# Retention and a mixture of experts on one core: other SBUF places for x and the first weights, and the two parts of an expert's first layer in two runs

## The chip, the cores and the metric

The kernel runs on one NeuronCore of a Trainium2 chip. Its time is the time of one execution on the device, in microseconds (us). The median of three executions before the change is 603.05 us (602.06 to 604.78).

The engines have short names here, as in the profile: PE is TensorE's matmul, PEld its load of the stationary operand, DVE is VectorE, ACT is ScalarE, POOL is GpSimd, SP is the queue that starts most DMA transfers.

## What is computed

The reference takes q, k and v of 8 batches, 8 heads, 576 positions and 64 channels. It computes retention, and sends each of the 4,608 resulting rows of 512 values through one of eight experts, the one whose gate logit is largest.

```
scores = scale * q @ k.T                     # per batch and head
ret = scores * Dmat                          # gamma ** (i - j) for i >= j, else 0
x = (ret @ v), heads side by side            # (4608, 512)

logits = x @ w_gate                          # (4608, 8)
e_idx = argmax(logits)
gate_w = softmax(logits)[e_idx]
eom = sigmoid(x @ w_output_gate)
for e in range(8):
    mask = e_idx == e
    h = maximum(x[mask] @ w1[e], 0.0)        # w1[e] is 512 x 1024
    ye = h @ w2[e]                           # w2[e] is 1024 x 512
    out[mask] = gate_w[mask] * eom[mask, e] * ye
```

## The kernel before

**Two stages.** The first, up to about 160 us, computes retention in 36 tiles of 128 rows and scatters the finished rows of x into a table in DRAM, sorted by expert. The second runs the eight experts. Each expert has room for 616 rows (`CAP`), in two parts: part 0 of 360 rows (`CA`) and part 1 of 256. Rows over 616 would go through a loop at the end.

**Numbers in two halves.** Every operand of an expert's matmuls is split into a high and a low half in a 32-bit format that one pass of PE takes (`F32R`): `xh` and `xl`, `w1h` and `w1l`, and so on. A product is the sum of three matmuls: high by high, and the two mixed ones.

**The first layer.** `mm1(e, part, fb)` makes block `fb` of 128 of the 1,024 hidden columns, for one part of expert `e`: four slices `k` of the 512 inputs by three products, 12 matmuls into one PSUM tile `h_ps`. The stationary operand is 128 columns of a first-weight tile; the moving operand is x transposed, 360 columns in part 0 and 256 in part 1. ACT then makes `hh`, the high half of the rectified result (L275), and DVE `hl`, its low half (L276). There are four buffers of `h_ps`.

**The second layer.** `mm2(e, t)` makes one of five row tiles (three of part 0, with 128, 128 and 104 rows, two of part 1): 24 matmuls, the hidden rows stationary, 512 columns of the second weights moving (L289). ACT scales the result (L294) and POOL scatters it into the output.

**Order.** The second stage is written out by hand, and each engine keeps the order of the code. For each expert after the first, sixteen `mm1` blocks alternate between the parts, then five `mm2` follow. Expert 0's part 0 runs ahead of the loop (L664 to L671, L753), so that its loop has only the eight blocks of part 1. Into the loop over `fb` are set: the loads, casts and subtractions of this expert's second weights (`load_w(2, ...)`), the loads of the next expert's x (`load_x`) and row numbers (`load_idx`), and half of the next expert's first weights; the other half and the transposes of x (`transp_hi`, DVE's L245) are set between the `mm2`. Weights are staged in three buffers `st`, x in five buffers `x_q`. SP takes all these loads in one queue, and a load waits there for its buffer.

**Places in SBUF.** A matmul reads two operands from SBUF: the moving one, and the next matmul's stationary one, which PEld loads meanwhile. Each is a run of 4-byte numbers in each partition. All tiles of a kind begin at the same place within 256 bytes, since their sizes and the slices are multiples of 256 B. In the built program the bytes are, modulo 256: first weights 128, second weights 64, x of part 0 64, x of part 1 64, hidden tiles of both parts 64. So x begins 64 B below the first weights (192 modulo 256) in both parts, and the second weights at the same place as the hidden tiles (0). Three unused tiles called `shift` set these places; before the change there are two of them, `shift1` of 192 B between first and second weights (L139) and `shift2` of 128 B ahead of x's first part (L161).

Of the kernel before, what the change touches and what calls it, by code (L numbers as in the profile page):

```python
# [10 lines left out]
F32 = mybir.dt.float32  # L11
# [15 lines left out]
P = 128  # L27
# [12 lines left out]
FB = F // P  # L40
# [8 lines left out]
def tile_retention_moe(  # L49
# [20 lines left out]
    wpool = ctx.enter_context(tc.tile_pool(name="wpool", bufs=1))  # L70
# [58 lines left out]

    W1, W2 = {}, {}

    def start_w(which, e, fp):
        src, shape = (w1, [P, KB, 256]) if which == 1 else (w2, [P, 2, DM])
        st = wst.tile(shape, F32, name="st")
        SP.dma_start(out=st, in_=src[e, fp].rearrange("p (a b) -> p a b", a=shape[1]))
        if which == 2 and not W2:
            wpool.tile([P, 48], F32, name="shift1")  # L139
        hi = wpool.tile(shape, F32R, name=f"w{which}h{fp}")  # L140
        lo = wpool.tile(shape, F32R, name=f"w{which}l{fp}")
        (W1 if which == 1 else W2)[e, fp] = (hi, lo)
        return st, hi, lo

    def hi_w(st, hi, lo):
        for h in range(2):
            k = slice(h * st.shape[1] // 2, (h + 1) * st.shape[1] // 2)
            A.copy(out=hi[:, k], in_=st[:, k])  # L148

    def lo_w(st, hi, lo, part=range(2)):  # L150
        for h in part:
            k = slice(h * st.shape[1] // 2, (h + 1) * st.shape[1] // 2)
            V.tensor_tensor(out=lo[:, k], in0=st[:, k], in1=hi[:, k].bitcast(F32), op=ALU.subtract)  # L153

    def load_w(which, e, fp):
        w = start_w(which, e, fp)
        hi_w(*w)
        lo_w(*w)
# [6 lines left out]
    pools = {"xt0": xta, "ht0": hpa}  # L165
# [14 lines left out]
    def load_x(e, t):  # L180

        XG[e, t] = pools["xq"].tile([P, 4, P], F32, name="x_q")
        o = e * NT + ROW0[t]
        for a in range(4):
            read(paced=e == 1 and a == 0, out=XG[e, t][32 * a:32 * a + 32],
                 in_=xs[o:o + P, P * a:P * a + P].rearrange("(u j) c -> j u c", u=4))

    def load_idx(e, part, first=None):
        ts = range(TA) if part == 0 else range(TA, CT)
        if e == 0 and part == 0:  # L190
            for t in ts:
                o, m = ROW0[t], ROWS[t]
                read(first=first, out=idx[0:m, e, t], in_=xs[o:o + m, DM:DM + 2].bitcast(I32))
        else:
            o = e * NT + ROW0[ts[0]]
            read(out=idx[:, e, ts[0]:ts[-1] + 1],
                 in_=xs[o:o + P * len(ts), DM:DM + 2].rearrange("(t p) w -> p t w", p=P).bitcast(I32))
# [29 lines left out]
    def transp(e, t):  # L227
        transp_lo(*transp_hi(e, t))

    def transp_hi(e, t):  # L230
        part, n = (0, TA * P) if t < TA else (1, CAP - CA)
        t0 = t if part == 0 else t - TA
        if (e, part) not in XT:
            pl = pools[f"xt{part}"]
            XT[e, part] = (pl.tile([P, KB, n], F32R, name=f"xh{part}"), pl.tile([P, KB, n], F32R, name=f"xl{part}"))
        m = ROWS[t] if e == 0 else P
        hi, lo = (a[:, :, P * t0:P * t0 + m] for a in XT[e, part])
        if e == 0:
            src = pools["x_ps"]()[:, :, :, 0:m]
            for k in range(KB):  # L240
                T.transpose(src[:, k // 2, k % 2, :], XG[e, t][0:m, k:DM:KB], ident[0:m, 0:m])
            hi, lo = (a.rearrange("p (b k) i -> p b k i", b=2) for a in (hi, lo))
        else:
            src = pools["xq"].tile([P, KB, P], F32, name="x_t", bufs=2)
            V.transpose(out=src.rearrange("p k (u j) -> p u k j", u=4),  # L245
                        in_=XG[e, t].rearrange("p u (i k) -> p u k i", k=KB))
        A.copy(out=hi, in_=src)
        return src, hi, lo

    def transp_lo(src, hi, lo):  # L250
        V.tensor_tensor(out=lo, in0=src, in1=hi.bitcast(F32), op=ALU.subtract)

    def mm1(e, part, fb):
        hidden(*mm1_products(e, part, fb))

    def mm1_products(e, part, fb):
        n = CA if part == 0 else CAP - CA
        xh, xl = XT[e, part]
        wh, wl = (a[:, :, P * (fb % 2):P * (fb % 2) + P] for a in W1[e, fb // 2])
        w = -(-n // P) * P  # L260
        hh = pools[f"ht{part}"].tile([P, w], F32R, name=f"hh{part}{fb}")[:, 0:n]
        hl = pools[f"ht{part}"].tile([P, w], F32R, name=f"hl{part}{fb}")[:, 0:n]
        HT[e, part, fb] = (hh, hl)
        ps = pools["ps_h"].tile([P, 512], F32, name="h_ps")[:, 0:n]
        j = 0
        for k in range(KB):
            for a, b in ((wh, xh), (wh, xl), (wl, xh)):
                i = T.matmul(ps, lhsT=a[:, k, :], rhs=b[:, k, 0:n], start=(j == 0), stop=(j == 3 * KB - 1))  # L268
                if j == 0:
                    pe[0] = i.ins  # L270
                j += 1
        return ps, hh, hl

    def hidden(ps, hh, hl):
        A.activation(out=hh, in_=ps, func=AF.Relu)  # L275
        V.scalar_tensor_tensor(out=hl, in0=ps, scalar=0.0, in1=hh.bitcast(F32), op0=ALU.max, op1=ALU.subtract)  # L276

    def mm2(e, t):
        part = 0 if t < TA else 1
        t0 = t if part == 0 else t - TA  # L280
        m = ROWS[t]
        n = slice(P * t0, P * t0 + m)
        ps = pools["ps_y"].tile([P, DM], F32, name="y_ps")[0:m]
        j = 0
        for fb in range(FB):
            wh, wl = (a[:, fb % 2, :] for a in W2[e, fb // 2])
            hh, hl = HT[e, part, fb]
            for a, b in ((hh, wh), (hh, wl), (hl, wh)):
                i = T.matmul(ps, lhsT=a[:, n], rhs=b, start=(j == 0), stop=(j == 3 * FB - 1))  # L289
                if j == 0:  # L290
                    pe[0] = i.ins
                j += 1
        y = pools["y"].tile([P, DM], F32, name="y")[0:m]
        A.activation(out=y, in_=ps, func=AF.Copy, scale=idx.bitcast(F32)[0:m, e, t, 1:2])  # L294
        G.indirect_dma_start(out=out, out_offset=bass.IndirectOffsetOnAxis(ap=idx[0:m, e, t, 0:1], axis=0),  # L295
                             in_=y, in_offset=None, bounds_check=NT - 1, oob_is_err=False)
# [268 lines left out]
    def weights(g):  # L565
        for w, at in wsched.items():
            if g == at[0]:
                wparts[w] = start_w(w[0], 0, w[1])
            if g == at[1]:
                hi_w(*wparts[w])  # L570
# [170 lines left out]
    def fill_slots(e):  # L741
        for f in fills[e]:
            G.memset(iw, 0.0)
            f()
# [18 lines left out]
    load_x(1, 1)  # L763
    for e in range(E):
        nx = e + 1 < E
        for fb in range(FB):
            if e > 0:
                mm1(e, 0, fb)
            mm1(e, 1, fb)
            if e > 0 and fb < 4:  # L770
                load_w(2, e, fb)
            if e == 0:

                if fb in (0, 2):
                    w.append(start_w(1, 1, 2 + fb // 2))
                if fb in (1, 3, 5):
                    load_x(1, 2 + fb // 2)
                if fb % 2 == 1:
                    hi_w(*w[fb // 2])
                    lo_w(*w[fb // 2])  # L780
            elif nx:
                if fb < CT:
                    load_x(e + 1, fb)
                if fb in (5, 6):
                    load_idx(e + 1, fb - 5)
                if fb in (5, 7):
                    load_w(1, e + 1, (fb - 5) // 2)
            if fb == (7 if e else 4) and e + 2 < E:
                fill_slots(e + 2)
        if e == E - 1:  # L790
            overflow_table()
        xw = {}
        for t in range(CT):
            if e > 0 or t >= TA:

                for u in range(CT) if e == 0 and t == TA else (t,) if e else ():
                    if nx:
                        xw[u] = transp_hi(e + 1, u)
                        if u > 0:
                            transp_lo(*xw[u - 1])  # L800
                        if u == CT - 1:
                            transp_lo(*xw[u])
                if e and nx and t in (1, 3):
                    load_w(1, e + 1, 2 + t // 2)
                mm2(e, t)
# [3 lines left out]
    with ExitStack() as octx:  # L809
# [3 lines left out]
        with tc.For_i(0, n, 1) as i:  # L813
            e = nc.values_load(ovt[0:1, 0, bass.ds(i, 1)], engines=[mybir.EngineType.SP], min_val=0, max_val=E - 1)
# [106 lines left out]
```

## Time and profile before

| | |
|---|---|
| median of three executions | 603.05 us |
| the profiled execution's own time | 606.21 us |
| its span, first to last instruction | 604.4 us |
| granted TensorE clock, mean | 0.997 |
| retention stage | up to about 159.5 us |
| experts | 159.5 to about 597.2 us |
| matmuls of the first layer (L268) | 1,536 |
| matmuls of the second layer (L289) | 960 |

The page gives busy time by engine. For matmuls that is not enough: they overlap, and each has a duration longer than its distance to the next. What a matmul costs is that distance, from its start to the start of the next one, called its pitch below. It is read from the timeline, in which each row is an instruction with its start, its duration and its operands.

### The profile page before, as it was taken

The numbers are of one execution on the slowest core, as the hardware profiler recorded it, in microseconds if no ns is written. First come the engines' busy times: TensorE is split into PE (matmuls) and PEld (weight loads), VectorE is DVE, ScalarE is ACT, GpSimd is POOL, SyncE is SP. The second block draws the span as 40 slices with busy tenths as digits, with TensorE's granted clock in tenths as the row PEclk, the third lists the DMA queues.
The fourth block names the chain that finished last, engine by engine and source line by source line (L and its number), as shares of the span: only waits on it lengthen the run. The fifth ranks groups of instructions, "written<-read, shape, count | busy, mean of one in ns | idle before, by whom it ended". The sixth has DMA issues, their size and how long they took to land. (4 is left out here: it accounts for less than half of the span.)

```text
span 604.4 us, 14010 instructions
## 1 busy us (share of the span) xinstructions
PE 593.0 (98%) x5692; PEld 530.2 (88%) x5692; DVE 330.5 (55%) x731; ACT 226.0 (37%) x502; POOL 189.1 (31%) x235
## 2 busy tenths in 40 slices
PE   8999999999999999999999999999999999999995
PEld 6888888888988999889979987997899799889974
DVE  3588788889650765625543563445265435626410
ACT  4534333234422544325332533443354234325110
POOL 2255454575565624116014301601340110110011
PEclk9999999999999999999999999999999999999998
DMA  8888889887226576435243634434362435221011
GB/s 315 303 307 297 318 300 329 301 278 237 91 106 190 169 207 178 145 102 158 94 133 117 175 109 145 120 122 140 98 192 88 134 96 146 94 84 52 1 39 41
DMA packets 54429, 98.97 MB, mean 164 GB/s; under 512 B 14903, under 2 KB 33336, under 8 KB 54364
## 3 DMA queue, kind: packets, MB, share of 16 engines
q1 hardware_dynamic: 44492, 75.42, 39.2%
q0 software_dynamic: 9440, 21.60, 9.7%
q8 instruction: 45, 0.74, 0.5%
q10 hardware_dynamic: 432, 1.05, 0.4%
q14 instruction: 20, 0.16, 0.1%
HBM read 76.45 MB, written 31.18 MB: 178 GB/s over the span
## 5 line engine op out<-in xcount | busy, mean ns | idle before, releaser
L268 PE MATMUL h_ps<-xh,w1h 128*128 128x360 f32 (+1 forms) x512 | 155.3, 303 | 0.0
L268 PE MATMUL h_ps<-xh,w1l 128*128 128x360 f32 (+1 forms) x512 | 155.0, 303 | 0.0
L268 PE MATMUL h_ps<-xl,w1h 128*128 128x360 f32 (+1 forms) x512 | 154.9, 303 | 0.0
L295 POOL DMA_INDIRECT out_dram<-y,idx x40 | 39.7, 993 | 314.1 <-ACT y L294 268.9
L276 DVE SCALAR_TENSOR_TENSOR hl<-h_ps,hh 128x360 fp32r<-128x360 f32 (+1 forms) x128 | 61.2, 478 | 127.9 <-ACT hh L275 112.5
L289 PE MATMUL y_ps<-w2h,hh 128*128 128x512 f32 (+1 forms) x320 | 124.9, 390 | 0.0
L289 PE MATMUL y_ps<-w2l,hh 128*128 128x512 f32 (+1 forms) x320 | 124.9, 390 | 0.0
L289 PE MATMUL y_ps<-w2h,hl 128*128 128x512 f32 (+1 forms) x320 | 124.6, 389 | 0.0
L275 ACT ACTIVATE hh<-h_ps 128x360 fp32r<-128x360 f32 (+1 forms) x128 | 54.7, 428 | 118.5 <-PE h_ps L268 113.1
L268 PEld LDWEIGHTS h_ps<-xl,w1h 128*128 128x128 f32 x512 | 96.3, 188 | 0.3
L268 PEld LDWEIGHTS h_ps<-xh,w1h 128*128 128x128 f32 x512 | 96.0, 188 | 0.3
L268 PEld LDWEIGHTS h_ps<-xh,w1l 128*128 128x128 f32 x512 | 96.0, 188 | 0.0
L294 ACT ACTIVATE y<-y_ps,idx 128x512 f32<-128x512 f32 (+1 forms) x40 | 27.5, 688 | 138.5 <-issue 90.1
L289 PEld LDWEIGHTS y_ps<-w2h,hl 128*128 128x128 f32 (+1 forms) x320 | 58.8, 184 | 14.1
L289 PEld LDWEIGHTS y_ps<-w2h,hh 128*128 128x128 f32 (+1 forms) x320 | 58.8, 184 | 13.8
L153 DVE TENSOR_TENSOR w1l<-st,w1h 128x512 fp32r<-128x512 f32 x64 | 44.5, 732 | 48.0 <-ACT w1h L148 44.2
L289 PEld LDWEIGHTS y_ps<-w2l,hh 128*128 128x128 f32 (+1 forms) x320 | 58.7, 184 | 13.6
L360 POOL TENSOR_TENSOR vp<-pk,con_sb 128x512 f32<-128x512 f32 x36 | 38.7, 1075 | 56.7 <-PE st_ps L400 35.1
L200 POOL DMA_INDIRECT xs<-zx,fill x42 | 45.9, 1094 | 7.1 <-issue 6.6
L200 POOL DMA_INDIRECT xs<-xgrp,sli x36 | 38.0, 1055 | 29.6 <-issue 10.5
L384 DVE TENSOR_TENSOR S_sb<-sc,con_sb 128x512 f32<-128x512 f32 x64 | 41.1, 683 | 9.5 <-PE sc L373 8.3
L153 DVE TENSOR_TENSOR w2l<-st,w2h 128x512 fp32r<-128x512 f32 x64 | 43.7, 721 | 2.3
(130 smaller groups left out, 683.7 us busy)
## 6 DMA issues: line engine op xcount, KB each, us to landing
st<-in_w_dram SPq DMA_DIRECT2D x64, 512.0 KB
pk<-in_pack_dram SPq DMA_DIRECT2D x32, 768.0 KB
x_q<-xs SPq DMA_DIRECT2D x140, 64.0 KB
kn<-in_krow_dram SPq DMA_DIRECT2D x13, 256.0 KB
pk<-in_pack_dram SPq DMA_DIRECT2D x4, 256.0 KB
pk<-in_pack_dram SPq DMA_DIRECT2D x2, 512.0 KB
x_g<-xs SPq DMA_DIRECT2D x4, 256.0 KB
xs<-zx,fill POOLq DMA_INDIRECT x42
```

The lines of the kernel that those rows point to most:

```text
L153: V.tensor_tensor(out=lo[:, k], in0=st[:, k], in1=hi[:, k].bitcast(F32), op=ALU.subtract)
L200: i = G.indirect_dma_start(out=xs, out_offset=bass.IndirectOffsetOnAxis(ap=at, axis=0), in_=x, in_offset=None, **({} if bound is None else ...
L268: i = T.matmul(ps, lhsT=a[:, k, :], rhs=b[:, k, 0:n], start=(j == 0), stop=(j == 3 * KB - 1))
L275: A.activation(out=hh, in_=ps, func=AF.Relu)
L276: V.scalar_tensor_tensor(out=hl, in0=ps, scalar=0.0, in1=hh.bitcast(F32), op0=ALU.max, op1=ALU.subtract)
L289: i = T.matmul(ps, lhsT=a[:, n], rhs=b, start=(j == 0), stop=(j == 3 * FB - 1))
L294: A.activation(out=y, in_=ps, func=AF.Copy, scale=idx.bitcast(F32)[0:m, e, t, 1:2])
L295: G.indirect_dma_start(out=out, out_offset=bass.IndirectOffsetOnAxis(ap=idx[0:m, e, t, 0:1], axis=0), in_=y, in_offset=None, bounds_check= ...
L360: G.tensor_tensor(out=vs[g], in0=pk[g][:, 2].rearrange("p (h d) -> p h d", h=H), in1=gk_sb[:, g % CPB].broadcast_to([P, H, D]), op=ALU.mult)
L384: V.tensor_tensor(out=v(S_sb[:, r].rearrange("p a i -> p (a i)")), in0=v(sc[:, r]), in1=cmat_sb[:, 0:2].rearrange("p c a i -> p a (c i)"). ...
```

## The change

The unused tile `shift1` (192 B) moves ahead of the first weights. They start 192 B later, at 64 modulo 256; the second weights stay where they are. A new unused tile `shift3` (64 B) in the pool of x's part 1, which grows down from the top, moves that part 64 B down, from 64 to 0. A new `shift4` (192 B) behind the hidden tiles of part 1 brings them back to 64. The result: x of part 0 is at 0 B from the first weights (it was 64 B below them), x of part 1 at 64 B below them (as before), the second weights at 0 B from the hidden tiles (as before).

The loop over the blocks becomes two: for experts 1 to 7 all eight blocks of part 0, with the second weights loaded at blocks 0, 2, 4 and 6; then for all experts the eight blocks of part 1, with the loads of the next expert as they were.

```diff
+    wpool.tile([P, 48], F32, name="shift1")
     W1, W2 = {}, {}
 
     def start_w(which, e, fp):
...
-        if which == 2 and not W2:
-            wpool.tile([P, 48], F32, name="shift1")
         hi = wpool.tile(shape, F32R, name=f"w{which}h{fp}")
...
             XT[e, part] = (pl.tile([P, KB, n], F32R, name=f"xh{part}"), pl.tile([P, KB, n], F32R, name=f"xl{part}"))
+            if (e, part) == (0, 1):
+                pl.tile([P, 16], F32, name="shift3")
...
         hl = pools[f"ht{part}"].tile([P, w], F32R, name=f"hl{part}{fb}")[:, 0:n]
+        if (e, part, fb) == (0, 1, FB - 1):
+            pools["ht1"].tile([P, 48], F32, name="shift4")
...
     for e in range(E):
         nx = e + 1 < E
+        for fb in range(FB if e > 0 else 0):
+
+            mm1(e, 0, fb)
+            if fb % 2 == 0:
+                load_w(2, e, fb // 2)
         for fb in range(FB):
-            if e > 0:
-                mm1(e, 0, fb)
             mm1(e, 1, fb)
-            if e > 0 and fb < 4:
-                load_w(2, e, fb)
             if e == 0:
 
                 if fb in (0, 2):
```

On ACT this is expert 2's first layer in the built program, from its first block; `hh` is a block's result, `w2h` and `w1h` the casts of staged weights. Before:

```order
L275 ACTIVATE hh_4189<-h_ps 128x360
L275 ACTIVATE hh_4206<-h_ps 128x256
L148 CAST w2h_4225<-st 128x512 x2
L275 ACTIVATE hh_4236<-h_ps 128x360
L275 ACTIVATE hh_4253<-h_ps 128x256
L148 CAST w2h_4272<-st 128x512 x2
L275 ACTIVATE hh_4283<-h_ps 128x360
L275 ACTIVATE hh_4300<-h_ps 128x256
```

And at the same place now:

```order
L279 ACTIVATE hh_4191<-h_ps 128x360
L148 CAST w2h_4210<-st 128x512 x2
L279 ACTIVATE hh_4216<-h_ps 128x360
L279 ACTIVATE hh_4233<-h_ps 128x360
L148 CAST w2h_4252<-st 128x512 x2
L279 ACTIVATE hh_4258<-h_ps 128x360
L279 ACTIVATE hh_4275<-h_ps 128x360
L148 CAST w2h_4294<-st 128x512 x2
```

The blocks of 360 columns follow one another, as they do on PE, and a cast of second weights stands behind every other one.

On SP, around the loads of expert 2's second weights, with `st` for staged weights (its last three loads of first weights stand ahead, in the same row), `x_q` for the next expert's x and `idx` for its row numbers. Before:

```order
L137 DMA st<-in_w_dram 128x1024 x4
L168 DMA x_q<-xs 32x4x128 x4
L137 DMA st<-in_w_dram 128x1024
L168 DMA x_q<-xs 32x4x128 x4
L137 DMA st<-in_w_dram 128x1024
L168 DMA x_q<-xs 32x4x128 x4
L137 DMA st<-in_w_dram 128x1024
L168 DMA x_q<-xs 32x4x128 x8
L168 DMA idx<-xs 128x3x2
```

Now:

```order
L139 DMA st<-in_w_dram 128x1024 x7
L168 DMA x_q<-xs 32x4x128 x20
L168 DMA idx<-xs 128x3x2
L139 DMA st<-in_w_dram 128x1024
L168 DMA idx<-xs 128x2x2
```

All twenty loads of the next expert's x now stand behind the last load of this expert's second weights, where the first twelve of them stood ahead of it. No instruction is added to any queue.

## The prediction

> **What bounds the kernel now.** I read the page's first two parts, then busy time by stage, then PE's timeline.
>
> ```profile
> span 604.4 us, 14010 instructions
> PE 593.0 (98%) x5692; PEld 530.2 (88%) x5692; DVE 330.5 (55%) x731; ACT 226.0 (37%) x502; POOL 189.1 (31%) x235
> ```
>
> PE is busy for 98% of the span. A share so high may still hide short waits, so the next view takes the first layer of single experts as stretches (columns: stretch, length, then busy time of PE, PEld, DVE, ACT, POOL, clock, DMA share and rate).
>
> ```profile
> 217.17:244.10 26.93, 26.93 (x193) 26.93 (x192) 13.70 (x25) 12.28 (x26) 10.36 (x12) 1.00 0.58 171
> 271.44:298.37 26.93, 26.93 (x193) 26.93 (x192) 13.70 (x25) 12.29 (x26) 9.76 (x11) 1.00 0.45 138
> 542.77:569.75 26.98, 26.98 (x195) 26.94 (x193) 12.40 (x23) 11.26 (x24) 0.98 (x1) 1.00 0.08 30
> ```
>
> In each, PE has no gap, at full clock; DVE and ACT are busy for half the time, and with the DMA share between 0.08 and 0.58 the length is the same to 0.05 us. Neither data nor another engine sets it: only how fast PE takes its own matmuls. So the pitch is what counts. It is read from starts in the timeline (start, duration, instruction), here at the first matmul of five successive blocks of expert 2:
>
> ```profile
> 271.44 0.33 PE L268 MATMUL h_ps<-xh,w1h 128*128 128x360 f32 x1
> ...
> 273.43 0.28 PE L268 MATMUL h_ps<-xh,w1h 128*128 128x256 f32 x1
> ...
> 274.85 0.33 PE L268 MATMUL h_ps<-xh,w1h 128*128 128x360 f32 x1
> ...
> 276.84 0.28 PE L268 MATMUL h_ps<-xh,w1h 128*128 128x256 f32 x1
> ...
> 278.21 0.32 PE L268 MATMUL h_ps<-xh,w1h 128*128 128x360 f32 x1
> ```
>
> Twelve matmuls of 360 columns take 1.99 us in both blocks. Twelve of 256 take 1.42 us in the first and 1.37 us in the second, though they are the same instructions with the same places modulo 256 B. So the pitch depends on what went before. Once it has settled, it is (later rows of the same view; the 256 columns, then the 360, then the second layer's 512):
>
> ```profile
> 290.63 0.28 PE L268 MATMUL h_ps<-xh,w1h 128*128 128x256 f32 x1
> ...
> 291.65 0.32 PE L268 MATMUL h_ps<-xh,w1h 128*128 128x360 f32 x1
> 291.81 0.33 PE L268 MATMUL h_ps<-xl,w1h 128*128 128x360 f32 x1
> 291.97 0.33 PE L268 MATMUL h_ps<-xh,w1l 128*128 128x360 f32 x1
> ...
> 293.64 0.28 PE L268 MATMUL h_ps<-xh,w1h 128*128 128x256 f32 x1
> ```
>
> ```profile
> 299.76 0.39 PE L289 MATMUL y_ps<-w2h,hh 128*128 128x512 f32 x1
> ...
> 308.82 0.39 PE L289 MATMUL y_ps<-w2l,hh 128*128 128x512 f32 x1
> ```
>
> 256 columns: 290.63 to 291.65 is nine pitches, 113.3 ns each. 512 columns: 299.76 to 308.82 is forty, 226.5 ns each. Both are 0.4425 ns a column. 360 columns: 291.97 to 293.64 is ten, 167 ns, or 0.464 ns a column; at 0.4425 it would be 159.3 ns. The first two after the switch, at 291.65 and 291.81, are 160 ns, and then the pitch climbs. So the 360-column blocks lose about 7 ns a matmul that the others don't, and lose it only after some matmuls: that looks like the two streams that PE reads from SBUF falling into step, not like a cost of 360 columns as such. They lie 64 B apart; so do those of the 256 columns, without the loss, and those of the 512 columns lie at 0 B.
>
> **The change part by part.**
>
> *Part 0 from 64 B below to 0 B.* Each of experts 1 to 7 has 8 × 12 = 96 matmuls of 360 columns, now 8 × 1.99 = 15.92 us. No row shows 360 columns at 0 B. From above: the top pitch that the settled blocks show is 167 ns, and a loss as large again on top of it would give 174 ns. From below: the fastest that a neighbouring row allows is the 159.3 ns at the others' rate. I take 159.4 ns, nearest to the second layer's row, which is the only one at 0 B: 96 × 159.4 = 15.30 us, 0.62 us less for each expert. At 174 ns it would be 16.70 us.
>
> *Part 1 stays 64 B below, but in a row.* Now a first block at 1.42 and seven at 1.37 make 11.01 us. Eight in a row are shown for expert 0:
>
> ```profile
> 194.96 0.28 PE L268 MATMUL h_ps<-xh,w1h 128*128 128x256 f32 x1
> ...
> 206.26 0.40 PE L289 MATMUL y_ps<-w2h,hh 128*128 128x512 f32 x1
> ```
>
> That is 96 pitches in 11.30 us, 117.7 ns: the slower of the two settled values, kept to the end. The faster, 113.3 ns, follows a 360-column block in seven of eight blocks of each later expert. Part 1's run will follow 360 columns too, but such as have left the state that they were in. I take 113.3 ns: 96 × 113.3 = 10.88 us, 0.13 us less. At 117.7 ns it is 11.30 us, 0.29 us more than now.
>
> *Sum for experts 1 to 7:* 15.30 + 10.88 = 26.18 us against 26.93, 0.75 us less, seven times: 5.25 us.
>
> *Expert 0.* Its eight blocks of part 0 gain 12 × 7 ns = 0.085 us each, but not all of it lasts:
>
> ```profile
> 173.31 0.18 PE L734 MATMUL t_ps<-cum,cbf_sb 128*128 128x8 bf16 x1 [0.53 <-DVE cum L518]
> ```
>
> Here PE waits 0.53 us for the last counts, which follow the retention's last matmuls. Those come after the second block; what four of the blocks between gain goes into this wait. I count four blocks: 0.34 us.
>
> *Second layer.* Its relation and its instructions are as before, so I count nothing. What could differ is how its first matmuls after the switch settle; after the switch at 291.65 that was 7 ns for two matmuls, so 0.1 us either way over seven experts.
>
> *The order on the other engines.* Added instructions: none. Moved: casts and subtractions of second weights to every other block of part 0, and SP's loads. In the stretch 217.1 to 244.1 the groups are (line, operation, count, busy us, mean ns, idle):
>
> ```profile
> L148 ACT CAST w2h<-st 128x512 fp32r<-128x512 f32 x8 | 4.5, 617 | 0.0
> L275 ACT ACTIVATE hh<-h_ps 128x360 fp32r<-128x360 f32 x8 | 3.8, 471 | 7.0 <-PE h_ps L268 6.5 <-issue 0.5
> ```
>
> ```profile
> L153 DVE TENSOR_TENSOR w2l<-st,w2h 128x512 fp32r<-128x512 f32 x8 | 5.2, 688 | 0.3
> L276 DVE SCALAR_TENSOR_TENSOR hl<-h_ps,hh 128x360 fp32r<-128x360 f32 x8 | 4.3, 532 | 7.0 <-ACT hh L275 7.0
> L276 DVE SCALAR_TENSOR_TENSOR hl<-h_ps,hh 128x256 fp32r<-128x256 f32 x7 | 3.0, 425 | 5.7 <-ACT hh L275 4.9 <-issue 0.8
> ```
>
> For two blocks of 360, 2 × 12 × 159.4 ns = 3.83 us of PE, DVE has 2 × 0.53 + 2 × 0.69 = 2.44 us to do and ACT 2 × 0.47 + 2 × 0.62 = 2.18. In part 1 two blocks are 2.72 us of PE; the pair with first weights in it costs DVE 2 × 0.43 + 2 × 0.69 = 2.24 us. Both hold, and four PSUM buffers even out single blocks. Behind the moved loads on SP wait the next expert's x, row numbers and first weights; they are wanted here:
>
> ```profile
> 246.50 2.06 DVE L245 STREAM_TRANSPOSE x_t<-x_q 128x512 f32<-128x512 f32 x2
> ...
> 262.51 1.29 DVE L153 TENSOR_TENSOR w1l<-st,w1h 128x512 fp32r<-128x512 f32 x2 [5.33 <-ACT w1h L148]
> ```
>
> ```profile
> 223.48 4.12 SPq L168 DMA_DIRECT2D x_q<-xs  x8
> ```
>
> Eight x loads take SP 4.1 us, so twenty take 10.3. The fourth second-weight load needs a staging buffer, free after the first pair's subtraction, some 4 us into the stage; x is then in about 15 us into it, and DVE first wants it 26 us in. The last first weights are ready at 263.8, 7.6 us before the next stage at 271.44; PE will want them at block 6 of part 0, 11.5 us into it, where it was 20.2. So 11 to 19 us of the PE's own stream hide all this, and the cost is nothing; with that cover gone, each us that x comes late is one of PE.
>
> **The sum.** 5.25 + 0.34 = 5.6 us less than the profiled execution's 606.21: 600.6. That execution lies 3.2 us above the median of 603.05; the gain is in pitches, which repeat from expert to expert, so the median moves by as much: **597.5 us**.
>
> **A rule of the skill.** The Trainium skill, TensorE: Matmul & The Clock Gate, "Step-by-step: what each phase is for", says that PE has two independent read ports and that loading the next weights takes no read bandwidth from the running matmul; its section "Back-to-back issue gap" would put 360 columns at an estimated 360/2.4 + 2.5 = 152.5 ns, wherever the operands lie. The trace has 160 to 167 ns, and 113.3 or 117.7 ns for one and the same 256. So I give more to a loss between the streams than to that rule, but it is the third rival below; by it the edit of places would bring nothing.
>
> **The rivals.**
>
> *Part 1 in the slower state (600.5 us).* The run settles at 117.7 ns: 7 × (11.30 − 10.88) = 3.0 us on top of the forecast. For it: the one run of eight that the trace has; a first block after the second layer and a settled 360 goes there as well (1.42 us at 273.43). Against: a 360-column stream without its loss should leave the other state behind.
>
> *0 B is worse for 360 columns (607.9 us, slower).* This is one mechanism: each matmul of part 0 finds the weight stream in step with it for longer. Its price at 174 ns is 16.70 + 10.88 = 27.58 us, 0.65 more for each expert, 4.55 for seven, and 0.34 for expert 0's four blocks. It decides from 167 ns on, (26.93 − 10.88)/96, or from 163 ns if part 1 is slow too. For it: at 0 B, with 104 columns loaded instead of 128, the second layer is slower, not faster:
>
> ```profile
> 309.29 0.39 PE L289 MATMUL y_ps<-w2h,hh 128*104 128x512 f32 x1
> ...
> 314.79 0.40 PE L289 MATMUL y_ps<-w2h,hh 128*128 128x512 f32 x1
> ```
>
> 24 pitches in 5.50 us, 229.2 ns against 226.5: 0 B is not free in itself. Against: even that is 0.448 ns a column, 161 ns for 360.
>
> *The places do nothing (602.7 us).* If 360 columns cost 167 ns in themselves, the run takes 16.0 us, part 1 10.88, together 0.05 us less: 0.35 in all; with part 1 slow, 605.7. For it: no row has one width at two relations. Against: the 160 ns after each switch.
>
> **How the numbers follow.** The forecast has 0.42, part 1 slow 0.22, 0 B worse 0.10, places without effect 0.15; 0.11 is left for a pitch between 160 and 164 ns or a wait that I haven't seen. The range is **594.8 to 605.5**: below, 158 ns for 360 columns (some 0.9 us further) with the 1 us by which the lowest of three executions lies under their median and a little more; above, places without effect and the 1.7 us by which the highest lies over it, or part 1 slow as well. About 0.5%, 3 us, is what a measurement can tell from no change. Faster by more: the forecast and half of what lies near 600, 0.53. Slower: 0 B worse and a part of the rest, 0.12. Within: 0.35.
>
> **What will show it.** Right: expert 2's eight blocks of 360 columns span 15.3 us, and its eight of 256 columns 10.9; the second layer's tiles still 5.44 to 5.50 us; no idle time before any L268 or L289. Wrong: 16.0 us or more for part 0 (places), 11.3 for part 1 (its state), or PE waiting for `xh` or `w1h` (the loads).

## The result, and the profile after

| | before | after |
|---|---|---|
| median of eight executions | 602.86 us (600.91 to 604.78) | 599.73 us (599.25 to 600.12) |
| the profiled execution's own time | 606.21 us | 600.12 us |
| its span | 604.4 us | 598.3 us |
| granted TensorE clock, mean | 0.997 | 0.996 |

The ratio of the medians is 0.9946, with a 95% interval of 0.9929 to 0.9962: faster by 0.5%, some 2.3 to 4.3 us. The prediction was 597.5 us, in a range of 594.8 to 605.5. The measured time lies in the range, but nearer to the first rival's 600.5.

The page of the changed kernel begins as that of before did:

```profile
span 598.3 us, 14014 instructions
PE 586.4 (98%) x5692; PEld 525.7 (88%) x5692; DVE 330.8 (55%) x731; ACT 227.0 (38%) x502; POOL 186.3 (31%) x235
```

PE still has all its 5,692 matmuls and still is busy for 98%. It is only done sooner. So where the time went is read by stages again. First the stretches of the kernel before that the prediction did not show: the retention stage, expert 0 (from its first matmul of the first layer to expert 1's), expert 1's second layer, and all experts from the first such matmul to the last of the second layer (length, then busy time of PE, PEld, DVE, ACT, POOL, clock, DMA share and rate).

```profile
0.00:159.51 159.51, 155.74 (x3173) 136.01 (x3174) 125.59 (x355) 63.54 (x178) 75.50 (x108) 1.00 0.81 285
159.51:217.17 57.66, 57.13 (x338) 51.46 (x336) 29.95 (x82) 20.33 (x43) 33.42 (x41) 1.00 0.54 168
244.10:271.44 27.34, 27.34 (x123) 22.05 (x122) 12.47 (x17) 8.89 (x16) 3.98 (x4) 1.00 0.39 124
159.51:596.93 437.42, 436.89 (x2521) 394.18 (x2520) 204.95 (x376) 161.81 (x324) 112.62 (x127) 1.00 0.39 122
```

The same stretches of the changed kernel, with expert 1's first layer as its two runs:

```profile
0.00:155.38 155.38, 151.71 (x3173) 133.95 (x3174) 127.26 (x355) 64.70 (x178) 75.34 (x108) 1.00 0.82 292
155.38:213.04 57.66, 56.55 (x337) 50.88 (x336) 29.99 (x82) 20.18 (x43) 34.04 (x41) 1.00 0.50 165
213.04:228.40 15.36, 15.36 (x97) 15.36 (x96) 8.21 (x15) 8.09 (x16) 10.64 (x12) 1.00 0.58 166
228.40:239.71 11.31, 11.31 (x99) 11.31 (x97) 5.29 (x11) 4.18 (x10) 0.00 (x0) 1.00 0.49 147
239.71:267.01 27.30, 27.30 (x122) 22.05 (x121) 12.49 (x17) 8.89 (x16) 3.98 (x4) 1.00 0.32 114
155.38:590.80 435.42, 434.31 (x2521) 391.73 (x2520) 203.58 (x376) 161.56 (x324) 110.00 (x127) 1.00 0.39 123
```

Four things are to be seen. The 360-column blocks of an expert now take 15.36 us (15.92 before). The 256-column blocks take 11.31 us: the larger of the two settled pitches (11.01 before, 10.88 expected). Expert 0 and the second layer are unchanged. And the profiled executions differ by 6.1 us, but the experts by 2.00 us only: the other 4.13 us are in the retention stage, 159.51 us in one profile and 155.38 in the other, with the same instructions. That stage varied between 154.1 and 160.3 us over the profiles of all kernels here, so the difference of the two profiles is not the gain. (On one chip alone the profiles differ there by 2.2 us at most, 158.1 to 160.3.) The before that was profiled, 606.21 us, is slower than every one of the eight before that were timed beside the changed kernel.

Expert 2, where the prediction said what would show it right, in the timeline (start, duration, instruction):

```profile
267.01 0.32 PE L272 MATMUL h_ps<-xh,w1h 128*128 128x360 f32 x1
...
282.38 0.28 PE L272 MATMUL h_ps<-xh,w1h 128*128 128x256 f32 x1
...
293.68 0.39 PE L293 MATMUL y_ps<-w2h,hh 128*128 128x512 f32 x1
```

From 267.01 to 282.38 are 96 pitches, 160.1 ns each; from 282.38 to 293.68 another 96, 117.7 ns each. All of experts 1 to 7 are like this. Added up from the starts of their blocks, the 360 columns take 107.53 us where they took 111.43 (3.90 less), the 256 columns 79.15 where they took 77.12 (2.03 more), and the second layers of all experts 218.46 where they took 218.58. With expert 0 at no change that is 3.90 − 2.03 + 0.12 = 1.99 us, the 2.00 of the stage.

### The profile page after: what moved, and what is told of

It is laid out like the page before. It is cut to its first block, busy times and chain, and to the rows that moved or that the text cites. A ratio compares the mean times of both kernels' runs of the same rounds, so it can differ in the third digit from the quotient of the medians.

```text
span 598.3 us, 14014 instructions
## 1 busy us (share of the span) xinstructions
PE 586.4 (98%) x5692; PEld 525.7 (88%) x5692; DVE 330.8 (55%) x731; ACT 227.0 (38%) x502; POOL 186.3 (31%) x235
## 5 line engine op out<-in xcount | busy, mean ns | idle before, releaser
L272 PE MATMUL h_ps<-xh,w1h 128*128 128x256 f32 (+1 forms) x512 | 154.7, 302 | 0.0
L272 PE MATMUL h_ps<-xh,w1l 128*128 128x256 f32 (+1 forms) x512 | 154.5, 302 | 0.0
L272 PE MATMUL h_ps<-xl,w1h 128*128 128x256 f32 (+1 forms) x512 | 154.5, 302 | 0.0
L280 DVE SCALAR_TENSOR_TENSOR hl<-h_ps,hh 128x256 fp32r<-128x256 f32 (+1 forms) x128 | 61.1, 477 | 129.1 <-ACT hh L279 125.7
L279 ACT ACTIVATE hh<-h_ps 128x256 fp32r<-128x256 f32 (+1 forms) x128 | 54.8, 428 | 116.9 <-PE h_ps L272 114.8
L153 DVE TENSOR_TENSOR w1l<-st,w1h 128x512 fp32r<-128x512 f32 x64 | 47.3, 776 | 48.0 <-ACT w1h L148 46.6
L364 POOL TENSOR_TENSOR vp<-pk,con_sb 128x512 f32<-128x512 f32 x36 | 37.5, 1041 | 52.9 <-PE st_ps L404 37.4
L200 POOL DMA_INDIRECT xs<-zx,fill x42 | 43.3, 1031 | 7.2 <-issue 6.5
```

The costliest lines, as they stand in the source:

```text
L200: i = G.indirect_dma_start(out=xs, out_offset=bass.IndirectOffsetOnAxis(ap=at, axis=0), in_=x, in_offset=None, **({} if bound is None else ...
L364: G.tensor_tensor(out=vs[g], in0=pk[g][:, 2].rearrange("p (h d) -> p h d", h=H), in1=gk_sb[:, g % CPB].broadcast_to([P, H, D]), op=ALU.mult)
```

## The experiments

The question is what each half of the change does, what a settled pitch depends on, and why the run of 256 columns has the larger of its two settled pitches, 117.7 and not 113.3 ns (what the prediction called its states). Places are given as before: where the moving operand begins from the stationary one, in bytes. Each diff is against the changed kernel, and each ratio is to the kernel before, timed on the same chip.

### The places without the order

```diff
-        for fb in range(FB if e > 0 else 0):
-            mm1(e, 0, fb)
-            if fb % 2 == 0:
-                load_w(2, e, fb // 2)
         for fb in range(FB):
+            if e > 0:
+                mm1(e, 0, fb)
             mm1(e, 1, fb)
+            if e > 0 and fb < 4:
+                load_w(2, e, fb)
```

> The new places with the old order: blocks of 360 and 256 columns alternate, x of part 0 at 0 B from the first weights. If the place sets the 360 columns' pitch (theory), they settle at 160 ns as in the changed kernel: 8 blocks take 15.36 us for an expert. If it was the run of equal blocks that did it (rival), they stay at 166 to 167 ns, 15.9 us. The 256 columns have the place that they had; if the block before them decides which of their two values they take, either is possible: 113.3 ns gives about 26.2 us for an expert's first layer and about 597.8 us in all, 117.7 ns gives 26.7 us and about 601 us.

It took 603.34 us against 606.07, a ratio of 0.9952 (0.9937 to 0.9967). Four successive blocks of expert 2 (360, 256, 360, 256 columns) and the experts' stage, as stretches:

```profile
269.71:271.64 1.93, 1.93 (x14) 1.92 (x13) 0.00 (x0) 0.69 (x1) 0.71 (x1) 1.00 0.00 0
271.64:273.05 1.41, 1.41 (x14) 1.41 (x13) 0.53 (x1) 0.47 (x1) 1.25 (x3) 1.00 0.41 158
273.05:274.97 1.92, 1.92 (x15) 1.92 (x13) 1.23 (x3) 1.41 (x3) 1.76 (x3) 1.00 0.40 158
274.97:276.38 1.41, 1.41 (x14) 1.41 (x13) 1.03 (x2) 0.47 (x1) 1.35 (x2) 1.00 0.02 0
157.89:593.50 435.61, 434.31 (x2521) 391.70 (x2520) 204.93 (x376) 161.76 (x324) 113.24 (x127) 1.00 0.41 123
```

Twelve matmuls of 360 columns take 1.92 us, 160.0 ns each, in every block; twelve of 256 take 1.41 us, the larger pitch, in every block too, though the order is the old one. The stage takes 435.61 us, 0.2 more than with the new order, as much as PE waits longer in expert 0 (1.3 us against 1.1). So the places bring the whole gain, and its loss on part 1 as well.

### The order without the places

The three `shift` edits are taken back and the two loops are kept.

> The old places with the new order: x of both parts 64 B below the first weights. Theory: the run of 360 columns stays at 166.7 ns, 16.0 us for an expert, and the run of 256 columns keeps the value it starts with; after a settled 360 it went to 117.7 ns before the change in each expert's first block, so 11.3 us, together 27.3 us for an expert, 2.6 us more in all than before: about 605.5 us. Rival: a run of equal blocks in itself makes them faster: 160 ns and 15.4 us without any change of places.

It took 608.64 us against 606.07, a ratio of 1.0043 (1.0027 to 1.006): slower. Expert 2's two runs and the experts' stage:

```profile
272.65:288.65 16.00, 16.00 (x98) 16.00 (x96) 8.30 (x15) 8.09 (x16) 9.07 (x11) 1.00 0.55 143
288.65:299.96 11.31, 11.31 (x98) 11.31 (x97) 5.21 (x11) 4.18 (x10) 0.00 (x0) 1.00 0.47 149
159.94:600.39 440.45, 439.50 (x2521) 396.78 (x2520) 203.75 (x376) 161.72 (x324) 110.61 (x127) 1.00 0.40 121
```

360 columns in a row settle at 16.00 / 96 = 166.7 ns, with none of the first pairs at 160 ns that each switch gave before; and part 1 is at 117.8 ns. The stage is 3.0 us longer than before (440.45 against 437.42). The order alone loses; with the new places it neither gains nor loses.

### The two runs exchanged

```diff
-            mm1(e, 0, fb)
+            mm1(e, 1, fb)
             if fb % 2 == 0:
                 load_w(2, e, fb // 2)
         for fb in range(FB):
-            mm1(e, 1, fb)
+            mm1(e, 0 if e > 0 else 1, fb)
```

> The changed kernel with the two runs of experts 1 to 7 exchanged: the eight blocks of 256 columns come first, right behind the second layer, then the eight of 360. Places as in the changed kernel. Theory that a run keeps the state in which it is entered: the 256 columns are entered from a 512-column stream instead of a 360-column one, so their pitch can change from 117.7 to 113.3 ns (as expert 0's run shows in the changed kernel, also behind the second layer), which would be 10.9 us instead of 11.3 us for an expert and 3 us less in all; the 360 columns are then entered from 256 columns and stay at 160.0 or go to 164.5 ns (15.4 or 15.8 us). Rival, the place alone sets the pitch: 117.7 and 160.0 ns as before, no change.

It took 604.34 us against 606.12, 0.997 (0.9951 to 0.9989). Expert 2's 256 columns and then its 360:

```profile
271.73:283.04 11.31, 11.31 (x97) 11.30 (x96) 6.87 (x14) 7.30 (x16) 9.27 (x11) 1.00 0.56 152
283.04:298.40 15.36, 15.36 (x98) 15.36 (x97) 6.34 (x12) 4.92 (x11) 0.18 (x1) 1.00 0.53 149
```

Entered from the second layer in place of the 360 columns, part 1 takes the larger pitch again, and part 0 keeps 160.0 ns. So it is not the 360-column run as such that leads into the larger pitch.

### Other places for x

Part 0 32 B above the first weights. It is the weights that move, 32 B down, under the same x; part 1 is moved along with them, and the second weights and the rest stay where they were:

```diff
-    wpool.tile([P, 48], F32, name="shift1")
+    wpool.tile([P, 40], F32, name="shift1")
...
+        if which == 2 and not W2:
+            wpool.tile([P, 8], F32, name="shift5")
...
-                pl.tile([P, 16], F32, name="shift3")
+                pl.tile([P, 24], F32, name="shift3")
...
-            pools["ht1"].tile([P, 48], F32, name="shift4")
+            pools["ht1"].tile([P, 40], F32, name="shift4")
```

> The changed kernel with x of part 0 at 32 B above the first weights instead of 0 B; part 1 stays 64 B below them, the second layer at 0 B. Theory of steps: 3.3 ns for 32 B, so 360 columns settle at 156.7 ns if so short a distance is within reach, and at 170.0 ns, the next step, if it is not: 2.2 us less or 6.7 us more over seven experts. Rival: only the 64 B in which the place was changed counts, not a finer part of it: 160.0 ns, no change.

It took 606.65 us, 1.0007 (0.9989 to 1.0024). Expert 2's run of 360 columns:

```profile
271.55:287.23 15.68, 15.68 (x97) 15.68 (x96) 8.26 (x15) 8.10 (x16) 8.96 (x11) 1.00 0.53 139
```

15.68 / 96 = 163.3 ns, in every block of experts 1 to 7: between the value at 0 B and that at 64 B. That is neither the 156.7 nor the 170.0 ns of the theory of steps (its reasoning stands with the second weights, below), nor the rival's unchanged 160.0.

Part 1 at 0 B (`shift3` removed, `shift4` of 64 numbers in place of 48), and part 1 32 B below (`shift3` of 8, `shift4` of 56):

> The changed kernel with x of part 1 at 0 B from the first weights too, instead of 64 B below. Theory: the place decides which pitches are possible; 64 B made 6.7 ns at 360 columns and 2.2 ns or more at 512. For 256 columns I have no row at 0 B: between 113.3 ns (10.9 us for an expert) and 120 ns (11.5 us). Rival, only the state at entry counts: 117.7 ns as now.

> The changed kernel with x of part 1 32 B below the first weights instead of 64 B. For 360 columns 32 B above cost 3.3 ns against 0 B. Theory that 64 B below is a good place for 256 columns which the run only enters wrongly: any other place has pitches of 117 ns or more, so no gain. Rival, that 64 B below is itself the trouble: one pitch, below 117 ns, in all blocks, expert 0 included.

They took 606.01 us, 0.9992 (0.9976 to 1.0008), and 604.84 us, 0.9982 (0.9966 to 0.9998). Expert 2's run of 256 columns, first at 0 B:

```profile
285.89:297.40 11.51, 11.51 (x98) 11.51 (x97) 5.29 (x11) 4.18 (x10) 0.00 (x0) 1.00 0.50 157
```

and at 32 B below:

```profile
285.80:297.16 11.36, 11.36 (x99) 11.36 (x97) 5.29 (x11) 4.18 (x10) 0.00 (x0) 1.00 0.52 160
```

At 0 B, 256 columns take 11.51 / 96 = 119.9 ns (120.0 in each of the later blocks), in expert 0 too: slower than either pitch at 64 B below. At 32 B below it is 118.3 ns on average, between 115 and 123 from one matmul to the next. So 0 B, the best of the three places tried for 360 columns, is the worst of the three for 256.

Is it the distance between the operands, or the place of one of them? For 256 columns it is not the place of one alone: with the first weights at 64 modulo 256, x at 0, 32 and 64 gives another result each time; and 64 B below was reached with the weights at 128, at 64 and, in the kernel with part 0 at 32 B, at 32, with no settled pitch but 113.3 and 117.7 ns. So there the distance counts. For 360 columns this is not shown, since x stayed where it was in all these kernels and only the weights moved.

### Other places for the second layer

Here the hidden tiles are the stationary operand, and the second weights move. The second weights 64 B up, so 64 B above the hidden tiles:

```diff
+        if which == 2 and not W2:
+            wpool.tile([P, 16], F32, name="shift5")
...
-    xta.tile([P, 32], F32, name="shift2")
+    xta.tile([P, 16], F32, name="shift2")
```

> The changed kernel with the second weights 64 B further, so at 64 B above the hidden tiles where they were at 0 B; all else keeps its place. Theory of steps: the settled pitches are 160.0 ns (360 columns, 0 B), 166.7 (360, 64 B below), 113.3 (256, 64 B below) and 226.7 (512, 0 B). 64 B moved the 360 columns by 6.7 ns, and if 6.7 ns for each 64 B below is taken away, all four are multiples of 13.3 ns: 12, 12, 8 and 17. So 512 columns at 64 B should settle at 220.0 ns, 6.7 ns less: some 6 us less in all, about 593.5 us. Rival: 0 B is right for a long stream and 64 B costs it as it cost the 360 columns: 233 ns, 6 us more. Second rival: the second layer does not depend on its place: 226.7 ns, no change.

It took 608.75 us, 1.0038 (1.0021 to 1.0056). Expert 1's two runs and its second layer:

```profile
217.67:233.45 15.78, 15.78 (x97) 15.78 (x96) 8.26 (x15) 8.10 (x16) 11.01 (x12) 1.00 0.60 162
233.45:244.35 10.90, 10.90 (x98) 10.90 (x97) 5.14 (x11) 4.14 (x10) 0.00 (x0) 1.00 0.52 151
244.35:271.92 27.57, 27.57 (x122) 22.06 (x121) 12.58 (x18) 8.89 (x16) 3.98 (x4) 1.00 0.35 113
```

512 columns settle at 228.9 ns here against 226.7, and a second layer takes 0.27 us more. So the theory of steps, with 220.0 ns, is wrong here too, and so are both rivals. The second row is the surprise: the first layer's operands lie where they lay, yet its 360 columns settle at 15.78 / 96 = 164.4 ns, and its 256 columns at 10.90 / 96 = 113.5, their smaller pitch. From expert 2 on, 360 stays at 164.4 and 256 is back at 117.8.

Two more kernels, with a single execution each, have the hidden tiles moved: in one, part 0's by 32 B up and part 1's by 32 B down (the new `shift6` of 8 numbers ahead of part 0's, `shift4` of 56); in the other, part 0's by 96 B up and part 1's by 64 B up (`shift6` of 24, `shift4` of 32). Beside one execution of the kernel before at 601.72 us they took 604.8 and 605.55.

> The changed kernel with the hidden tiles moved: those of part 0 32 B up and those of part 1 32 B down, so that the second weights lie 32 B below the hidden tiles in the first three row tiles of each expert and 32 B above them in the last two. Theory that the place decides which pitches are possible, and that 0 B, at 226.7 ns, is not the best for 512 columns: one of the two is under 226.7 ns; 220 ns would be 2.9 us less over the first three tiles' 432 ordinary matmuls. Rival: 0 B is the best for 512 columns, as 64 B above was 228.8 ns, and both are at 227 to 233 ns.

> The same with the hidden tiles of part 0 96 B up and those of part 1 64 B up: the second weights lie 96 B below the hidden tiles in the first three row tiles of each expert and 64 B below in the last two. Same theories: one of the two under 226.7 ns, or both at 227 to 233 ns. 64 B below is half of 128 B as 64 B above was (228.8 ns): if only the distance within 128 B counts, the last two tiles are at 228.8 ns.

Expert 1's second layer with the tiles moved by 32 B:

```profile
239.83:267.81 27.98, 27.98 (x122) 22.05 (x121) 12.55 (x17) 8.90 (x16) 3.98 (x4) 1.00 0.35 112
```

and by 96 and 64 B:

```profile
240.34:268.34 28.00, 28.00 (x123) 22.10 (x121) 12.56 (x17) 8.90 (x16) 3.98 (x4) 1.00 0.35 111
```

Both are 0.7 us longer than the 27.30 at 0 B. With 32 B to either side the pitch is 233.3 ns; in the other kernel it is 234.2 for part 0's tiles and 233.3 for part 1's. The second of these has its weights 64 B below the hidden tiles, and the experiment before it, 64 B above, had 228.9: so it is not the distance alone. Either its side counts, or the place of one operand by itself: the weights were moved in the one, the hidden tiles in the other, and no run separates the two. There as well the 360 columns change without having been moved, here in expert 2:

```profile
268.34:284.12 15.78, 15.78 (x97) 15.78 (x96) 8.27 (x15) 8.11 (x16) 9.00 (x11) 1.00 0.56 143
```

That is 164.4 ns again, and the 256 columns are at 117.8 ns in expert 1 and at 113.3 from expert 2 on.

### An extra matmul at the entry of the run

Same instructions and same places had given both 113.3 and 117.7 ns. If the entry decides, a single extra matmul ahead of the run should be able to change it, at a cost of about 0.1 us. Its result is overwritten by the first matmul behind it. It was tried with 128 columns in experts 1 to 7:

```diff
         j = 0
+        if e > 0 and part == 1 and fb == 0:
+            T.matmul(ps[:, 0:128], lhsT=wh[:, 0, :], rhs=xh[:, 0, 0:128], start=True, stop=True)
         for k in range(KB):
```

> The changed kernel with one additional matmul of 128 columns ahead of the run of 256 columns in experts 1 to 7; the matmul behind it overwrites what it wrote. It costs 60 to 115 ns for each expert, 0.4 to 0.8 us in all. Theory that a run keeps the state in which it is entered: this shifts the streams at entry, and may send the run to 113.3 ns, 0.42 us less for an expert and 3 us less in all; if so the 256 columns are at 113.3 ns in all eight blocks of all seven experts, with nothing else changed. Rival, the place alone sets the pitch: 117.7 ns, and 0.4 to 0.8 us more.

It took 604.57 us against 606.12, 0.9969 (0.9953 to 0.9986): no help. Expert 2's run with its extra matmul:

```profile
286.37:297.79 11.42, 11.42 (x100) 11.42 (x99) 5.29 (x11) 4.19 (x10) 0.00 (x0) 1.00 0.52 162
```

11.42 us is 117.8 ns for the 96 matmuls and 0.11 us for the extra one. One width doesn't say much, so the next kernel has another extra matmul in each expert (first and last column given; 16 begins 64 B further on):

```diff
+KICK = {1: (0, 32), 2: (0, 64), 3: (0, 96), 4: (0, 192), 5: (16, 144), 6: (0, 160), 7: (0, 256)}
...
+        if part == 1 and fb == 0 and e in KICK:
+            c0, c1 = KICK[e]
+            T.matmul(ps[:, 0:c1 - c0], lhsT=wh[:, 0, :], rhs=xh[:, 0, c0:c1], start=True, stop=True)
```

> The changed kernel with one additional matmul ahead of each run of 256 columns, as with the kick of 128 columns before it, but another in each expert: 32, 64, 96, 192 columns in experts 1 to 4, 128 columns from 64 B further on in expert 5, 160 in expert 6, 256 in expert 7; the matmul behind it overwrites what it wrote. Theory that a run keeps the state in which it is entered: some of the seven runs are at 113.3 ns (10.9 us), others at 117.7 ns (11.3 us), each from its first block to its last, with the same places in all; the kick of 256 columns is an ordinary matmul of the run and stays at 117.7 ns. Rival, that after 360 columns at 0 B only one value is to be had: all seven at 117.7 ns.

It took 598.64 us in a single execution (before: 601.72). The seven runs, experts 1 to 7 in order, extra matmul included:

```profile
227.37:238.78 11.41, 11.41 (x98) 11.41 (x98) 5.29 (x11) 4.19 (x10) 0.00 (x0) 1.00 0.48 150
281.47:292.49 11.02, 11.02 (x99) 11.02 (x98) 5.26 (x11) 4.14 (x10) 0.00 (x0) 1.00 0.57 170
335.17:346.18 11.01, 11.01 (x100) 11.01 (x98) 5.27 (x11) 4.14 (x10) 0.00 (x0) 1.00 0.53 168
388.86:399.87 11.01, 11.01 (x99) 11.01 (x98) 5.26 (x11) 4.14 (x10) 0.00 (x0) 1.00 0.56 167
442.55:453.97 11.42, 11.42 (x100) 11.42 (x98) 5.30 (x11) 4.18 (x10) 0.00 (x0) 1.00 0.47 144
496.66:508.07 11.41, 11.41 (x99) 11.41 (x98) 5.29 (x11) 4.18 (x10) 0.00 (x0) 1.00 0.43 145
550.76:562.23 11.47, 11.47 (x100) 11.43 (x99) 4.10 (x9) 3.15 (x8) 0.00 (x0) 1.00 0.01 1
```

Extra matmuls of 64, 96 and 192 columns put the run at 113.3 ns, those of 32, 128, 160 and 256 leave it at 117.8. Each width stands in one expert only here, but 128, from the first column, gave 117.8 in all seven experts of the experiment before, and 96 is tried in all seven next. The run has two pitches at one place, and what stands at its entry chooses; after the first few matmuls it keeps the one chosen to its end.

### The extra matmul of 96 columns in every expert

The lines in `mm1` are those of the last experiment, with another table:

```diff
+KICK = {e: (0, 96) for e in range(1, 8)}
```

> The changed kernel with the kick of 96 columns ahead of the run of 256 columns in all of experts 1 to 7. Theory that a run keeps the state in which it is entered, and that 96 columns enter the faster one: all seven runs at 113.3 ns, as expert 3 showed, about 11.0 us with the kick where they are 11.3 us; 0.30 us less for an expert, 2.1 us less than the changed kernel: a ratio to the kernel before of about 0.991. Rival, that what came out in one expert was chance and not the kick: some experts at 117.7 ns, and a ratio near the changed kernel's 0.995.

It took 602.88 us against 606.70, a ratio of 0.9928 (0.9906 to 0.9951). The entry of expert 2's run in the timeline:

```profile
286.73 0.21 PE L273 MATMUL h_ps<-xh,w1h 128*128 128x96 f32 x1
286.78 0.35 PE L276 MATMUL h_ps<-xh,w1h 128*128 128x256 f32 x1
286.96 0.28 PE L276 MATMUL h_ps<-xl,w1h 128*128 128x256 f32 x1
```

The extra matmul is not as cheap as its own 0.05 us: the one behind it starts early and then takes 0.18 us to the next, so the two take 0.23 us, about 0.11 more than an ordinary one. The seven extra matmuls of the last experiment are alike in this: each pair takes 227 to 234 ns, from 32 columns to 256.

Expert 2's two runs and the experts' stage as stretches:

```profile
271.37:286.73 15.36, 15.36 (x97) 15.36 (x96) 8.21 (x15) 8.11 (x16) 8.89 (x11) 1.00 0.54 139
286.73:297.74 11.01, 11.01 (x100) 11.01 (x98) 5.27 (x11) 4.15 (x10) 0.00 (x0) 1.00 0.54 168
160.23:593.39 433.16, 432.25 (x2529) 389.59 (x2527) 203.63 (x376) 161.63 (x324) 109.33 (x127) 1.00 0.41 123
```

All seven runs are at 113.3 ns, and the stage is 2.26 us shorter than the changed kernel's (433.16 against 435.42): 0.30 us in each of the seven runs, extra matmul included, and 0.2 us of shorter waiting in expert 0. Seven more matmuls make the stage shorter. Its ratio to the kernel before is the lowest of those timed, but its interval overlaps the changed kernel's, which was timed beside other executions of the kernel before (606.70 us here, 602.86 there): that it beats that one is shown by the stage, not by the timed ratios.

## Why the prediction came out as it did

*The bound.* Right. No stretch of experts 1 to 7 in the changed kernel has idle time of PE, and what moved the time was the pitch.

*Part 0 at 0 B.* The lever was right, since the new place takes the loss away, and the size nearly so; that the loss comes of two streams falling into step was not shown. The pitch is 160.0 ns, where the step took 159.4, so 15.36 us for an expert and not 15.30. Over the seven experts that is 3.90 us less, of 4.3 expected. The places alone show it with the old order, and 163.3 ns at 32 B above and 166.7 at 64 B below show that at one and the same width the pitch goes with the place. It is not the place alone: with only the second layer's operands moved, 0 B had 164.4 ns. With that the rivals "0 B is worse" and "the places do nothing" fell. The rule that was weighed against the trace, in the Trainium skill, TensorE: Matmul & The Clock Gate, "Step-by-step: what each phase is for", does not explain it: by two read ports that are independent, a place would change nothing, and it changed the pitch of the same 360 columns from 166.7 to 160.0 ns. The 152.5 ns that the prediction worked out from another section of that page, "Back-to-back issue gap", rests on a formula that the Trainium skill gives there for a single matmul and not for a stream of loads and matmuls; here no run of 360 columns settles below 160.0.

*Part 1 in a row.* This is the step that failed, though the time came out in the range: "Part 1's run will follow 360 columns too, but such as have left the state that they were in. I take 113.3 ns". Every run of part 1 in experts 1 to 7 is at 117.7 ns: 79.15 us in all against 77.12, 2.0 us more than before where 0.9 less was expected, and that is about the 3.0 us that the first rival had priced. Of the two grounds in the text, the run that the trace had, expert 0's, gave the right value, but by luck: in the changed kernel that very run takes the other one, 113.3 ns, at the same distance. The reason given was wrong: part 0 did leave its loss, and part 1 did not follow it into the smaller pitch, neither behind such a run, nor alternating with such blocks, nor ahead of it. The runs show in its place that the entry chooses, in a way that a nearby row doesn't tell: with seven different extra matmuls ahead of it, three runs went to 113.3 ns. Why these three is open.

*Expert 0.* Expected 0.34 us less; it takes 57.66 us in both. Three parts changed. Its 360 columns at 0 B settle at about 164.5 ns and not at 160.0, which is still 2 ns less than before; in its last two blocks these 24 pitches take 3.94 us, 164.2 ns each:

```profile
169.93 0.33 PE L272 MATMUL h_ps<-xh,w1h 128*128 128x360 f32 x1
...
173.87 0.40 PE L293 MATMUL y_ps<-w2h,hh 128*128 128x512 f32 x1
```

Its 256 columns now have the smaller pitch; the timeline of the changed kernel has their first and the matmul behind them:

```profile
191.26 0.28 PE L272 MATMUL h_ps<-xh,w1h 128*128 128x256 f32 x1
...
202.15 0.39 PE L293 MATMUL y_ps<-w2h,hh 128*128 128x512 f32 x1
```

That is 10.89 us where it was 11.30. But the wait for the counts, 0.53 us before, took what had been gained:

```profile
169.63 0.18 PE L738 MATMUL t_ps<-cum,cbf_sb 128*128 128x8 bf16 x1 [1.11 <-DVE cum L522]
```

PE's busy time in expert 0 did fall, from 57.13 to 56.55 us, more than the 0.34 expected; the wait, 0.58 us longer, took it all in this profile. The prediction said that a part would go into this wait. But the wait is not simply gain given back: it was 1.0 us in the order alone, whose places are the old ones, and in the kernels with new places it lay anywhere between 0.5 and 1.6 us. The kernel with the extra matmul of 128 columns, whose expert 0 is that of the changed kernel, had a wait of 0.5 us, and its expert 0 took 57.09:

```profile
159.81:216.90 57.09, 56.55 (x337) 50.87 (x336) 30.01 (x82) 20.17 (x43) 33.19 (x41) 1.00 0.53 167
```

In the kernel with seven different extra matmuls the same expert 0 waited 1.3 us and took 57.89. So by the profiles expert 0 lies anywhere from 0.6 us less to 0.2 us more than before, and a single one can't tell where.

*Second layer and moved loads.* Right: nothing. The second layers differ by 0.12 us of 218, and PE waits for neither `xh` nor `w1h`.

*The sum.* By pitches 2.0 us less, of 5.6 expected; of the missing 3.6, 2.9 are the pitch of part 1, 0.4 part 0's size, and 0.3 expert 0. The measured median moved by 3.1 us (2.3 to 4.3), about 1 us more than the stage. This is not explained by any pitch, and it is luck for the forecast, whose mechanism brought 2.0 us. Expert 0's wait could hold up to 0.6 us of it, and the retention stage, which differs by up to 6 us between the profiles here, more than the rest; no experiment was on either. Other kernels show such differences both ways: against the kernel before, the places alone gained 2.7 us by the timed medians and 1.8 in the stage, and the kernel with 96 columns 3.8 by the medians and 4.3 in the stage. So this stays open.

## What to carry to other kernels

Where a stage is nothing but matmuls, read the pitch from starts over a whole run, not from durations or from busy shares: a loss of 7 ns in each matmul shows in no wait. Before relying on a place of the operands, measure it for that width, since the best of the places tried for one width was the worst of them for another here. And where one instruction stream shows two settled pitches, don't infer which of them a new order will get: try it, with a small matmul ahead of the run as a cheap lever.

## What the runs showed of the hardware that was not expected

| moving columns | its place from the stationary operand, and the settled pitch |
|---|---|
| 360 | 0 B: 160.0 or 164.5 ns; 32 B above: 163.3; 64 B below: 166.7 |
| 256 | 64 B below: 113.3 or 117.7; 32 B below: 118.3; 0 B: 120.0 |
| 512 (128 columns loaded) | 0 B: 226.7; 64 B above: 228.9; 32 B either side: 233.3; 64 B below: 233.3; 96 B below: 234.2 |

PE's stream of matmuls has a memory. A change in the second layer's places alone moved the first layer's 360 columns from 160.0 to 164.4 ns, over eight blocks without a pause, and an extra matmul of 96 columns made the run of 96 behind it shorter by more than the 0.11 us that it cost: 11.01 us for all 97, where the 96 alone took 11.31. That the two streams which PE reads from SBUF meet there would fit this, and is argued, not shown: no record of the trace tells of a read that waits. Five of the steadiest values (113.3, 120.0, 160.0, 166.7 and 226.7 ns) are 17, 18, 24, 25 and 34 times 6.67 ns. But 117.8 ns, which varies no more (117 to 119 from one matmul to the next), is no multiple of it, so this is no rule, and where the step comes from is open too.
